# Starting a chunk's first four w_in tiles around the last x matmuls, and loading two w_out rows earlier

## The chip, the cores and the metric

One core of one Trainium2 chip runs the whole program. The metric is the device time in microseconds (us); the profile shows one execution and its span, which is some 1.8 us shorter than the time. A program on one core is timed in rounds: kernel and kernel before on the same chip, in turn.

## The reference, cut to what matters

```python
# q, k, v: (8, 8, 576, 64) float32; w_in: (512, 2048); w_out: (2048, 512)
q_s = softmax(q, axis=-1)                    # over head_dim
k_s = softmax(k, axis=2)                     # over the sequence
kv  = einsum('bhsd,bhse->bhde', k_s, v)      # 64 x 64 for each head
x   = einsum('bhsd,bhde->bhse', q_s, kv)     # then (B*S, H*D) = (4608, 512)
out = gelu_exact(x @ w_in) @ w_out
```

## The kernel before

Batch b's first 512 tokens make chunk b; the rest of all batches make chunk 8. For each chunk TensorE does, in order: kv (72 small 64x64 matmuls, two groups of two head pairs), x (8 matmuls on quarters of the array), h (16 w_in tiles of four 128x128x512 matmuls, each followed by a Gelu on ScalarE) and y (64 w_out matmuls into four banks). The change touches only the seam between chunk 0 and chunk 1. There chunk 0's y runs with the w_out row tiles t outermost, all four banks open, because w_out is still being loaded; the kv and x of batch 1 are put between the last y matmuls:

```python
    for t in range(12):
        y_part(t, range(J))                  # 4 matmuls, one for each y bank
    tp_step(1, 0)
    tp_step(1, 1)
    load(3)
    cast_wo(3, wo[3], 2, 1, "s")             # ScalarE casts row 2, then row 3
    cast_wo(3, wo[3], 3, 1, "s")
    y_part(12, range(J))
    y_part(13, range(J))
    kv_mm(1, 0)                              # 36 matmuls: pairs 0, 1
    kv_norm(1, 0)                            # VectorE: reciprocal, multiply -> kvc
    y_part(14, range(J))
    x_tile(1, 0, psum_a, "a")
    x_tile(1, 1, psum_h, "h")
    x_mm(1, 0)                               # 4 matmuls: pairs 0, 1
    kv_mm(1, 1)
    x_evac(1, 0, "s")                        # "s": ScalarE, else VectorE
    x_evac(1, 1, "s")
    kv_norm(1, 1)
    y_part(15, range(J))
    y_out(0, yps[0], 0)
    y_out(0, yps[1], 1, "s")
    # ... x tiles of pairs 2, 3 ...
    x_mm(1, 1)
    x_evac(1, 2)
    x_evac(1, 3, "s")
    y_out(0, yps[2], 2)
    y_out(0, yps[3], 3)
    h_phase(1, {12: [lambda: cast_v_all(2)]}, groups={0: 2})
```

The last loads of batch 1 and of w_out are issued in this order on one queue:

```python
    wo.append(load_wo(3))                    # its rows 0 and 1
    for hp in range(3):
        load_v1(hp)                          # 288 KB each
    load_wo_row(wo[3], 2)                    # 256 KB: w_out rows of t = 14
    load_v1(3)
    load_wo_row(wo[3], 3)                    # t = 15
```

The softmax here doesn't subtract the row's maximum and nothing guards it: scores larger than these inputs give would overflow.

## Time and profile before

| | before |
|---|---|
| time, median of 3 | 279.8 us (279.69 to 279.89) |
| span of the profiled execution | 278.4 us |
| TensorE (PE) busy | 269.5 us, 97% |
| ScalarE (ACT), VectorE (DVE), GpSimd (POOL) busy | 57%, 36%, 12% |
| all waits that the profile finds for PE | 4.3 us, none between 24 and 50 us |

A timeline line gives start, length, engine, line of the kernel, operation, what is written from what, shapes and the number of instructions merged; in brackets stands how long the engine had been idle and what ended that. The lines themselves are in the prediction.

### The profile page before, as it was taken

Reading aid. Unit: us, or ns where it says so; the run is one execution under the profiler, and the core shown is the slowest. Engines: PE = TensorE matmul, PEld = TensorE weight load, DVE = VectorE, ACT = ScalarE, POOL = GpSimd, SP = SyncE. Lnnn points to the kernel's source line nnn. Section 1 sums busy time; section 2 is a strip of 40 time slices with the busy share of each in tenths; the row PEclk is TensorE's granted clock in tenths of the full one; section 3 lists DMA queues with packets and bytes.
Section 4 is the critical chain, followed back from the end, with each engine's and each line's share of the span. In section 5 each row is a group of like instructions: output and inputs, shape, how many; then the busy total and the mean of one; then the engine's idle time right before and its main releaser. Section 6 shows DMA issues by size and latency. Waiting matters only on the chain.

```text
span 278.4 us, 4542 instructions
## 1 busy us (share of the span) xinstructions
PE 269.5 (97%) x1896; PEld 126.1 (45%) x1924; DVE 100.5 (36%) x151; ACT 158.4 (57%) x246; POOL 33.6 (12%) x25
## 2 busy tenths in 40 slices
PE   7799999999999999999999999999999999999995
PEld 3344454444444444444444444444444444444443
DVE  1877474309753540183008400651015200130012
ACT  3867666689377816691569346943683363136400
POOL 1620050002020220004000500050005000000000
PEclk9999999999999999999999999999999999999999
DMA  7999999963992139702981199117501500120033
GB/s 237 399 403 432 398 398 408 398 250 86 302 348 61 54 110 274 283 38 79 257 343 41 40 228 395 41 56 189 115 0 75 151 2 0 75 78 0 0 78 77
DMA packets 44980, 50.10 MB, mean 180 GB/s; under 512 B 20384, under 2 KB 29856, under 8 KB 44704
## 3 DMA queue, kind: packets, MB, share of 16 engines
q1 hardware_dynamic: 44560, 49.39, 52.9%
q10 hardware_dynamic: 400, 0.43, 0.6%
q8 instruction: 15, 0.25, 0.4%
q14 instruction: 5, 0.04, 0.1%
HBM read 36.70 MB, written 9.44 MB: 166 GB/s over the span
## 4 chain that ended last, share of the span: by engine, by line
PE 94%; DMA 2%; issue 1%; DVE 1%; POOL 1%; ACT 0%; POOLq 0%
PE ps L321 44%; PE ps L331 43%; PE kv L188 2%; DMA f<-in_q_dram 2%; PE ps L278 2%; PE ps L356 1%; POOL e L222 1%; PE pair L321 1%; PE ps L239 1%; ACT e L145 0%; DVE qsum L220 0%; PE ps L283 0%; DVE kvc L202 0%; PE tp L239 0%; PE ps L440 0%
## 5 line engine op out<-in xcount | busy, mean ns | idle before, releaser
L321 PE MATMUL ps<-xT,wi_bf 128*128 128x512 bf16 x557 | 124.2, 379 | 0.6
L331 PE MATMUL ps<-wo_bf,g 128*128 128x512 bf16 x543 | 122.1, 379 | 1.6 <-issue 1.1
L326 ACT ACTIVATE g<-ps 128x512 bf16<-128x512 f32 x142 | 83.7, 597 | 67.4 <-PE ps L321 67.4
L321 PEld LDWEIGHTS <-wi_bf 128*128 128x128 bf16 x576 | 56.2, 98 | 67.9 <-issue 0.2
L331 PEld LDWEIGHTS <-g 128*128 128x128 bf16 x560 | 53.9, 98 | 64.3 <-issue 0.4
L339 DVE COPY y_sb<-ps 128x512 f32<-128x512 f32 x34 | 23.3, 686 | 80.9 <-PE ps L331 77.8
L222 POOL TENSOR_TENSOR e<-e,recq 128x2048 bf16<-128x2048 bf16 (+1 forms) x9 | 25.7, 2856 | 177.6 <-DVE recq L221 149.5
L162 DVE CAST v_aug<-f 128x576 bf16<-128x576 f32 x25 | 17.1, 745 | 47.2 <-DMA f<-in_v_dram 47.2
L220 DVE TENSOR_REDUCE qsum<-e 128x16 f32<-128x1024 bf16 (+1 forms) x13 | 21.0, 1619 | 15.0 <-ACT e L145 15.0
L304 ACT CAST xT<-ps 128x512 bf16<-128x512 f32 x18 | 9.8, 588 | 26.1 <-PE ps L278 16.6
L145 ACT ACTIVATE e<-f 128x512 bf16<-128x512 f32 (+1 forms) x42 | 20.5, 556 | 3.7 <-DMA f<-in_q_dram 3.5
L150 ACT ACTIVATE ek<-f 128x2304 bf16<-128x2304 f32 (+1 forms) x10 | 17.1, 1726 | 0.4 <-DMA f<-in_k_dram 0.4
L302 DVE CAST xT<-ps 128x512 bf16<-128x512 f32 x17 | 11.0, 686 | 17.1 <-PE ps L278 14.1
L79 ACT ACT_TABLE_LOAD x9 | 11.5, 1283 | 2.8 <-issue 2.7
L440 PE MATMUL ps<-zeros 128*128 128x512 f32 (+1 forms) x16 | 8.7, 697 | 1.5 <-DVE zeros L474 1.5
L145 ACT ACT_TABLE_LOAD x7 | 9.0, 1283 | 0.1
L407 DVE CAST wi_bf<-w 128x512 bf16<-128x512 f32 x12 | 7.3, 663 | 2.2 <-DMA w<-in_moe_w_in_dram 1.9
L188 PEld LDWEIGHTS <-ek 64*64 64x64 bf16 x576 | 6.4, 105 | 2.7 <-issue 0.7
L188 PE MATMUL kv<-v_aug,ek 64*64 64x65 bf16 x576 | 6.8, 193 | 0.4 <-DVE kvc L202 0.4
L222 DVE TENSOR_TENSOR e<-e,recq 128x1024 bf16<-128x1024 bf16 x4 | 6.4, 1595 | 0.1
L278 PE MATMUL ps<-qT,kvc 64*64 64x512 bf16 x62 | 5.4, 389 | 0.4 <-DVE kvc L202 0.4
L440 PEld LDWEIGHTS ps<-zeros 128*128 128x128 f32 x14 | 3.3, 244 | 5.4 <-issue 4.0
(39 smaller groups left out, 49.6 us busy)
## 6 DMA issues: line engine op xcount, KB each, us to landing
out_dram<-y_sb SPq DMA_DIRECT2D x32, 256.0 KB, 2.4
f<-in_k_dram SPq DMA_DIRECT2D x6, 1152.0 KB, 9.8
f<-in_v_dram SPq DMA_DIRECT2D x6, 1152.0 KB, 11.6
f<-in_q_dram SPq DMA_DIRECT2D x6, 1024.0 KB, 7.3
w<-in_moe_w_in_dram SPq DMA_DIRECT2D x6, 512.0 KB, 8.9
f<-in_v_dram SPq DMA_DIRECT2D x8, 288.0 KB, 6.6
f<-in_q_dram SPq DMA_DIRECT2D x4, 512.0 KB, 9.1
w<-in_moe_w_out_dram SPq DMA_DIRECT2D x2, 1024.0 KB, 12.5
```

The costliest lines, as they stand in the source:

```text
L79: nc.scalar.activation(out=scr[:, 1:2], in_=scr[:, 0:1], func=func)
L145: nc.scalar.activation(out=dst[:, i], in_=src[:, u], func=AF.Exp)
L150: nc.scalar.activation(out=ek[b % 2][:, i:i + n], in_=st[b]["kf"][:, i:i + n].rearrange("p x (n d) -> p x n d", n=NS), func=AF.Exp,)
L162: eng.tensor_copy(out=o, in_=i)
L188: nc.tensor.matmul(ps[c, place[hp], 0:D + 1], ek[b % 2][pr, hp, n, :], v_aug[b % 2][pr, hp, n, 0:D + 1], start=(n == 0), stop=(n == NS - 1),)
L220: nc.vector.reduce_sum(out=qsum, in_=eq[:, :, hs, :], axis=AX.X)
L222: eng.tensor_tensor(out=eq[:, :, hs, :], in0=eq[:, :, hs, :], in1=recq.unsqueeze(3).to_broadcast([128, J, w, D]), op=ALU.mult,)
L321: nc.tensor.matmul(ps, wi_bf[:, dm, t * 128:(t + 1) * 128], xT[:, dm, :], start=(dm == 0), stop=(dm == NDM - 1),)
L326: nc.scalar.activation(out=g[:, t, :], in_=ps, func=AF.Gelu)
L331: nc.tensor.matmul(ps, st[c]["g"][:, t, j * 128:(j + 1) * 128], wo_bf[:, t, :], start=(t == 0), stop=(t == NDF - 1),)
L339: nc.vector.tensor_copy(out=y_sb, in_=ps)
L440: nc.tensor.matmul(ps, z[:, 0:128], z, start=True, stop=True)
```

## The change

Its intent: give TensorE work of chunk 1 that needs only the first two head pairs, so that the normalization of the other two and the copies of their x lie beside matmuls; and have row 3 of the last w_out block on chip earlier, since two of its matmuls now come earlier. Cut to its core:

```diff
-    for hp in range(3):
+    for hp in range(2):
         load_v1(hp)
     load_wo_row(wo[3], 2)
+    load_wo_row(wo[3], 3)
+    load_v1(2)
     load_v1(3)
-    load_wo_row(wo[3], 3)
 ...
     y_part(14, range(J))
+    y_part(15, (0, 1))
     x_mm(1, 0)
     kv_mm(1, 1)
+    y_out(0, yps[0], 0)
     x_evac(1, 0, "s")
-    x_evac(1, 1, "s")
+    x_evac(1, 1)
     kv_norm(1, 1)
-    y_part(15, range(J))
-    y_out(0, yps[0], 0)
     y_out(0, yps[1], 1, "s")
+    y_part(15, (2, 3))
+    h_begin(1)
+    hps = ...                     # two "h" banks, two "y" banks
+    for t in range(2):
+        h_mm(1, hps[t], t, (0, 1))         # the early w_in matmuls
+    y_out(0, yps[2], 2, "s")
+    y_out(0, yps[3], 3)
     x_mm(1, 1)
-    x_evac(1, 2)
-    x_evac(1, 3, "s")
-    y_out(0, yps[2], 2)
-    y_out(0, yps[3], 3)
-    h_phase(1, {12: [...]}, groups={0: 2})
+    x_evac(1, 2, "s")
+    x_evac(1, 3)
+    for t in range(2, 4):
+        h_mm(1, hps[t], t, (0, 1))
+    for t in range(4):
+        h_mm(1, hps[t], t, (2, 3))
+        h_gelu(1, hps[t], t)
+    h_phase(1, {12: [...]}, t1=4)
```

More of the change, by code (lines that the diff above doesn't have):

```diff
@@ L304, in x_evac, with h_begin, h_mm, h_gelu @@
             nc.scalar.copy(out=st[b]["xT"][:, hp, :], in_=ps)
-    def h_phase(c, ins, groups={}, banks={}):
-        g = moe_sb.tile([128, NDF, M], BF16, tag="g", bufs=1)
-        st[c]["g"] = g
-        xT = st[c]["xT"]
-        t1 = 0
+    def h_begin(c):
+        st[c]["g"] = moe_sb.tile([128, NDF, M], BF16, tag="g", name="g", bufs=1)
+    def h_mm(c, ps, t, dms):
+        for dm in dms:
+            nc.tensor.matmul(
+                ps, wi_bf[:, dm, t * 128:(t + 1) * 128], st[c]["xT"][:, dm, :],
+                start=(dm == 0), stop=(dm == NDM - 1),
+            )
+    def h_gelu(c, ps, t):
+        nc.scalar.activation(out=st[c]["g"][:, t, :], in_=ps, func=AF.Gelu)
+    def h_phase(c, ins, groups={}, banks={}, t1=0):
+        if t1 == 0:
+            h_begin(c)
         while t1 < NDF:
@@ L320, in h_phase @@
                 for ps, t in zip(pss, ts):
-                    nc.tensor.matmul(
-                        ps, wi_bf[:, dm, t * 128:(t + 1) * 128], xT[:, dm, :],
-                        start=(dm == 0), stop=(dm == NDM - 1),
-                    )
+                    h_mm(c, ps, t, (dm,))
             for ps, t in zip(pss, ts):
-                nc.scalar.activation(out=g[:, t, :], in_=ps, func=AF.Gelu)
+                h_gelu(c, ps, t)
                 for f in ins.get(t, []):
@@ L565 @@
     kv_mm(1, 1)
+    y_out(0, yps[0], 0)
     x_evac(1, 0, "s")
-    x_evac(1, 1, "s")
+    x_evac(1, 1)
     kv_norm(1, 1)
-    y_part(15, range(J))
-    y_out(0, yps[0], 0)
     y_out(0, yps[1], 1, "s")
+    y_part(15, (2, 3))
+    h_begin(1)
+    hps = [psum_h.tile([128, M], FP32, tag="h", name="ps") for t in range(2)]
+    hps += [psum_y.tile([128, M], FP32, tag="y", name="ps") for t in range(2)]
+    for t in range(2):
+        h_mm(1, hps[t], t, (0, 1))
+    y_out(0, yps[2], 2, "s")
+    y_out(0, yps[3], 3)
     x_tile(1, 2, psum_a, "a")
@@ L574 @@
     x_mm(1, 1)
-    x_evac(1, 2)
-    x_evac(1, 3, "s")
-    y_out(0, yps[2], 2)
-    y_out(0, yps[3], 3)
-    h_phase(1, {12: [lambda: cast_v_all(2)]}, groups={0: 2})
+    x_evac(1, 2, "s")
[5 more added lines that the diff above has]
+        h_gelu(1, hps[t], t)
+    h_phase(1, {12: [lambda: cast_v_all(2)]}, t1=4)
     exp_q(2, parts=2)
```

## The prediction

> **What bounds the kernel now.** I read first the page's busy times, then the waits of the TensorE alone, then the timeline of 41 to 45.6 us, where chunk 0 ends and chunk 1 begins, because the diff touches nothing else. First the page's row of busy times and two pieces of the chain that ended last in order of time (start, length, what); then every wait that the profile finds for PE, in the whole span:
>
> ```profile
> PE 269.5 (97%) x1896; PEld 126.1 (45%) x1924; DVE 100.5 (36%) x151; ACT 158.4 (57%) x246; POOL 33.6 (12%) x25
> ...
> 28.70 8.42 PE ps L331 x39
> ```
> ```profile
> PE ps L440 <- DVE zeros L474: 1.5, 1, 1.5
> PE ps L331 <- issue: 1.1, 7, 0.2
> PE ps L239 <- POOL e L222: 0.9, 1, 0.9
> PE kv L188 <- DVE kvc L202: 0.4, 1, 0.4
> PE ps L278 <- DVE kvc L202: 0.4, 1, 0.4
> ```
>
> PE is busy 97% of 278.4 us, and all its waits together are 4.3 us: 1.5 + 0.9 + 0.4 + 0.4 of them belong to batch 0's start (before 15 us), and 1.1 to seven pauses of 0.2 us. "Busy" alone would not prove a full pipe, so the rate is checked: 39 matmuls of 512 columns in 8.42 us are 0.216 us each. None of the waits lies between 24 and 50 us. So in the changed stretch the time is the sum of PE's issue intervals, and any gain must come from one of those being longer than it needs to be.
>
> The stretch itself, from the timeline (start, length, engine, line, operation, count; in brackets idle time before it), then a comparison piece from batch 2:
>
> ```profile
> 41.61 0.48 PE L188 MATMUL kv<-v_aug,ek 64*64 64x65 bf16 x36
> 41.65 0.67 POOL L162 CAST v_aug<-f 128x576 bf16<-128x576 f32 x1 [0.73 <-DMA f<-in_v_dram]
> 42.02 1.04 PE L331 MATMUL ps<-wo_bf,g 128*128 128x512 bf16 x3
> 42.25 0.62 ACT L435 CAST wo_bf<-w 128x512 bf16<-128x512 f32 x1 [0.77 <-DMA w<-in_moe_w_out_dram]
> 42.36 0.29 DVE L202 TENSOR_TENSOR kvc<-kv,rec 128x128 bf16<-128x128 f32 x1
> 42.99 0.41 PE L278 MATMUL ps<-qT,kvc 64*64 64x512 bf16 x4
> 43.23 0.51 PE L188 MATMUL kv<-v_aug,ek 64*64 64x65 bf16 x36
> 43.44 1.07 ACT L304 CAST xT<-ps 128x512 bf16<-128x512 f32 x2 [0.58 <-PE ps L278]
> 43.67 1.04 PE L331 MATMUL ps<-wo_bf,g 128*128 128x512 bf16 x4
> 44.01 0.29 DVE L202 TENSOR_TENSOR kvc<-kv,rec 128x128 bf16<-128x128 f32 x1
> 44.22 0.68 DVE L339 COPY y_sb<-ps 128x512 f32<-128x512 f32 x1
> 44.40 0.60 ACT L341 COPY y_sb<-ps 128x512 f32<-128x512 f32 x1
> 44.64 0.40 PE L278 MATMUL ps<-qT,kvc 64*64 64x512 bf16 x1
> 44.64 0.40 PE L278 MATMUL xx<-qT,kvc 64*64 64x512 bf16 x1
> ...
> 44.98 3.84 PE L321 MATMUL ps<-xT,wi_bf 128*128 128x512 bf16 x16
> 45.09 0.69 DVE L302 CAST xT<-ps 128x512 bf16<-128x512 f32 x1 [0.20 <-PE xx L278]
> 45.12 0.59 ACT L304 CAST xT<-xx 128x512 bf16<-128x512 f32 x1
> ```
> ```profile
> 66.52 4.91 PE L331 MATMUL ps<-wo_bf,g 128*128 128x512 bf16 x22 [0.16 <-issue]
> 71.36 0.63 PE L278 MATMUL ps<-qT,kvc 64*64 64x512 bf16 x8
> ```
>
> The reader is to see whether x waits for its kv. It looks as if it could: kvc is ready at 42.65 (42.36 + 0.29) and x starts at 42.99; again 44.30 and 44.64. But the four w_out matmuls ahead of x need 4 x 0.216 + 0.01 (the first one after small matmuls is 0.01 longer) = 0.87 us, and x comes 0.97 us after the first of them, 0.09 to 0.10 more. In batch 2, where kvc was ready long before, 22 w_out matmuls need 22 x 0.216 = 4.75 us, and x comes 71.36 - 66.52 = 4.84 us after the first: the same 0.09. So that 0.09 is a fixed price for going from whole-array matmuls to quarter-array ones, not a wait. Nothing waits here that could be hidden.
>
> **What the Trainium skill says.** "TensorE: Matmul & The Clock Gate", section "Back-to-back issue gap", gives a warm gap of N/2.4 + 2.5 ns, 216 ns for 512 columns; the trace agrees (0.216). "TensorEngine Tiling (Array Packing)", section "Key Properties", says that changing the tiling mode drains the engine; the trace agrees, at 0.09 us for each such entry. "Perfetto Trace Analysis", section "Matmuls", wants independent groups to rotate through PSUM banks so that an evacuation overlaps the next group; the four early w_in tiles do that, and the cost to check is whether their banks are evacuated in time. "DMA: Bandwidth & Descriptors", section "Two DMAs through the same engine are not ordered", says that descriptors of one queue start in order; this is why I take the rows of w_out to land in the order of issue, as rows 2, v 3, row 3 did (casts at 40.86, 41.65, 42.25).
>
> **The change, part by part.** No instruction is added or taken away: 8 w_out matmuls of t = 14 and 15, 8 x matmuls, 72 kv matmuls, 16 matmuls of four w_in tiles, four copies of x, four of y. Only their order differs.
>
> PE before, by starts: kv at 41.61; 0.41 to y14 (42.02); 0.97 to x01 (42.99); 0.24 to kv (43.23); 0.44 to y15 (43.67); 0.97 to x23 (44.64); 0.34 to h (44.98); 16 h matmuls, 16 x 0.216 + 0.01 = 3.46; the fifth w_in tile starts at 48.44.
> PE after: kv at 41.61; 0.41; six y matmuls, 0.97 + 2 x 0.216 = 1.40, x01 at 43.42; 0.24, kv at 43.66; 0.44, the last two y at 44.10; 4 h matmuls from 44.10 + 0.01 + 2 x 0.216 = 44.54; (2 + 4) x 0.216 + 0.10 = 1.40 puts x23 at 45.50; 0.34, h again at 45.84; 12 x 0.216 + 0.01 = 2.60; the fifth tile at 48.44.
> The number of entries into quarter-array mode is the same, so the sum is the same: 0.00 us, if nothing new waits.
>
> Now the new waits, with durations of the same rows; a semaphore takes about 0.05 us (x01 ends at about 43.40, ACT's copy starts at 43.44). Successive copies start 0.48 us apart on ACT (1.07 - 0.59) and 0.60 on DVE (1.28 for two of 0.68 further on in the timeline).
> - ACT: copy of x0 at 43.42 + 0.45 = 43.87, ends 44.46, ready for PE at 44.51; the first early h wants it at 44.54. Fits by 0.03. Copy of y bank 1 at 44.35, ends 44.95, ready 45.00; tile 1's first matmul, which takes that bank, wants it at 44.54 + 2 x 0.216 = 44.97. Late by 0.03. Copy of y bank 2 at 44.83 to 45.43, wanted at 45.84: in time.
> - DVE: y bank 0 is complete at about 43.27, its copy runs 43.32 to 44.00, x1's copy from 43.92 to 44.61, ready 44.66, wanted at 44.76: in time. kv's normalization follows at about 44.53 and ends about 45.03, wanted at 45.50: in time. y bank 3 until about 45.7, wanted at about 46.3: in time.
> - x2 and x3: copies at 45.50 + 0.45 = 45.95 to 46.6, wanted at 45.84 + 0.01 + 4 x 0.216 = 46.71: in time by about 0.1.
> - Loads: row 3 (256 KB) moves ahead of v 3 and v 2, so its cast runs about 1.4 us earlier, near 40.8 to 41.5; it is now wanted at 42.02 + 0.01 + 4 x 0.216 = 42.90, where the old cast end (42.25 + 0.62 = 42.87) would have been on the edge. v 2 and v 3 land some 0.6 us later (256 KB at about 400 GB/s); v 3's cast would then end near 42.32 + 0.6 = 42.9, wanted at 43.66: in time.
> Sum: 0.00 of work + 0.03 of wait = +0.03 us, which PE carries to the end because it never idles later.
>
> **Rivals.** (1) The change hides a wait and gains. The most it could win is the two x stages: 0.34 from x23 to h and 0.10 ahead of it, so 0.4 us, 279.4. Against it: those intervals are the mode change and the streaming of x itself, and remain. (2) Evacuation becomes the bound: ACT now has to copy x0, y1 and y2 in a row beneath 1.4 us of PE work, with margins of 0.03 us. If each copy came 0.1 to 0.2 us later than I place it, PE would stand 0.1 to 0.4 us: about 280.1. For it: the thin margins; against it: ACT is idle before 43.44 and its copies repeat to the nanosecond level. (3) v 2 and v 3 come late by more than their 0.7 us of margin, since the queue is saturated there (about 390 to 410 GB/s): kv and all behind it would slip by 0.3 to 0.8 us, about 280.4. Against it: only 256 KB passes them.
>
> **Range and chances.** Predicted 279.8 us. Runs of before spread over 0.2 us (279.69 to 279.89); rival 1 gives the lower edge, 279.4, and rivals 2 and 3 the upper, 280.3. 2% are 5.6 us; nothing in this stretch is that large, and only an unforeseen lost transfer or a slower chip could do it. Faster 0.005, same 0.98, slower 0.015.
>
> **What would show it.** In the changed trace: the x matmuls of pairs 0 and 1 about 0.43 us later and those of 2 and 3 about 0.86 us later than before; the four early h matmuls ahead of the latter without a gap over 0.05 us; the fifth w_in tile within 0.1 us of 48.44; ACT's cast of row 3 before 42 us; no new row among PE's waits above 0.2 us. I am wrong if the fifth tile starts more than 0.2 us from 48.44 or if a difference arises later than that tile, which would mean that the order of loads or of copies reaches further than I see.

## The result, and the profile after

The changed kernel takes 279.94 us (median of 6, 279.63 to 280.02), before 279.88 us (6 runs). The ratio is 1.0001, 95% interval 0.9988 to 1.0014: the same. A ratio here is the mean time of one kernel's fast runs over that of the other's of the same rounds, so not quite the ratio of the medians.

From the page and the timeline of the changed kernel (its w_out line is now L339, its w_in line L311):

```profile
PE 269.3 (97%) x1896; PEld 126.0 (45%) x1924; DVE 100.4 (36%) x151; ACT 158.3 (57%) x246; POOL 33.5 (12%) x25
```
```profile
39.72 1.26 ACT L443 CAST wo_bf<-w 128x512 bf16<-128x512 f32 x2 [0.66 <-DMA w<-in_moe_w_out_dram]
41.16 1.37 POOL L162 CAST v_aug<-f 128x576 bf16<-128x576 f32 x2 [1.36 <-DMA f<-in_v_dram]
41.29 0.48 PE L188 MATMUL kv<-v_aug,ek 64*64 64x65 bf16 x36
41.70 1.47 PE L339 MATMUL ps<-wo_bf,g 128*128 128x512 bf16 x5
42.99 0.69 DVE L347 COPY y_sb<-ps 128x512 f32<-128x512 f32 x1 [0.66 <-PE ps L339]
43.10 0.41 PE L278 MATMUL ps<-qT,kvc 64*64 64x512 bf16 x4
43.34 0.51 PE L188 MATMUL kv<-v_aug,ek 64*64 64x65 bf16 x36
43.55 0.59 ACT L304 CAST xT<-ps 128x512 bf16<-128x512 f32 x1 [2.57 <-PE ps L278]
43.78 0.60 PE L339 MATMUL ps<-wo_bf,g 128*128 128x512 bf16 x2
44.04 1.08 ACT L349 COPY y_sb<-ps 128x512 f32<-128x512 f32 x2
44.22 0.81 PE L311 MATMUL ps<-xT,wi_bf 128*128 128x512 bf16 x3
44.39 0.29 DVE L202 TENSOR_TENSOR kvc<-kv,rec 128x128 bf16<-128x128 f32 x1
45.18 0.40 PE L278 MATMUL ps<-qT,kvc 64*64 64x512 bf16 x1
45.52 3.20 PE L311 MATMUL ps<-xT,wi_bf 128*128 128x512 bf16 x14
```

PE's rows follow each other without a bracket, as before: nothing waits. (Counts of 5 and 3 where the program has 6 and 4 are missing records.) Everything is some 0.32 us earlier than in the first trace, because chunk 0 itself began earlier. So I measure from the first kv matmul, and use two rulers. The **stretch** runs from the first kv matmul of batch 1 to the first w_out matmul of chunk 1, by the starts of single matmuls: 17.195 us before, 17.195 us after. The **tail** runs from the start of the last matmul to the end of the span. Between the two lie 215.93 or 215.94 us in every trace, so whatever the stretch loses or gains reaches the end.

By step: x01 (pairs 0 and 1) started 1.81 us after the kv group (43.10 - 41.29), before 1.38; x23 at 3.89, before 3.03; the fifth w_in tile at 6.835 in both (by the starts of its first matmul, 48.123 - 41.288 and 48.443 - 41.608).

### The profile page after: what moved, and what is told of

The parts are those of the page before. It is cut to its first block, busy times and chain, and to the rows that moved or that the text cites. A ratio compares the mean times of both kernels' runs of the same rounds, so it can differ in the third digit from the quotient of the medians.

```text
span 278.1 us, 4543 instructions
## 1 busy us (share of the span) xinstructions
PE 269.3 (97%) x1896; PEld 126.0 (45%) x1924; DVE 100.4 (36%) x151; ACT 158.3 (57%) x246; POOL 33.5 (12%) x25
## 4 chain that ended last, share of the span: by engine, by line
PE 92%; DMA 4%; issue 1%; POOL 1%; ACTq 0%; SPq 0%; DVE 0%
PE ps L339 43%; PE ps L311 43%; DMA w<-in_moe_w_in_dram 3%; DMA touch<-in_moe_w_in_dram 2%; PE kv L188 2%; PE ps L278 1%; PE ps L364 1%; PE pair L311 1%; POOL wi_bf L412 1%; PE ps L283 0%; PE ps L239 0%; ACTq L468 0%; PE tp L239 0%; SPq L400 0%; ACTq L101 0%
## 5 line engine op out<-in xcount | busy, mean ns | idle before, releaser
L311 PE MATMUL ps<-xT,wi_bf 128*128 128x512 bf16 x557 | 124.3, 379 | 0.6
L339 PE MATMUL ps<-wo_bf,g 128*128 128x512 bf16 x543 | 122.1, 379 | 1.6 <-issue 1.1
L311 PEld LDWEIGHTS <-wi_bf 128*128 128x128 bf16 x576 | 56.1, 98 | 68.2 <-POOL wi_bf L412 0.8
L339 PEld LDWEIGHTS <-g 128*128 128x128 bf16 x560 | 53.9, 98 | 64.3 <-issue 0.4
L347 DVE COPY y_sb<-ps 128x512 f32<-128x512 f32 x33 | 22.7, 686 | 81.2 <-PE ps L339 78.1
L441 DVE CAST wo_bf<-w 128x2048 bf16<-128x2048 f32 (+1 forms) x4 | 4.4, 1090 | 3.8 <-DMA w<-in_moe_w_out_dram 3.8
```

What stands on the lines that cost most here:

```text
L311: nc.tensor.matmul(ps, wi_bf[:, dm, t * 128:(t + 1) * 128], st[c]["xT"][:, dm, :], start=(dm == 0), stop=(dm == NDM - 1),)
L339: nc.tensor.matmul(ps, st[c]["g"][:, t, j * 128:(j + 1) * 128], wo_bf[:, t, :], start=(t == 0), stop=(t == NDF - 1),)
L347: nc.vector.tensor_copy(out=y_sb, in_=ps)
```

## The experiments

All kernels gave correct outputs. Twelve ran. Here is what the two rulers show in each; "kv" is the start of the first kv matmul, that is, how late PE reached the stretch in that execution:

| run | kv, us | stretch, us | tail, us | time, us (before in the same rounds) |
|---|---|---|---|---|
| before | 41.61 | 17.195 | 3.68 | 279.88 (with the changed kernel) |
| changed kernel | 41.29 | 17.195 | 3.73 | 279.94 (279.88) |
| before_again | 41.13 | 17.197 | 3.70 | 279.75, one run (279.81) |
| loads_only | 41.36 | 17.194 | 3.75 | 280.05, one run (279.81) |
| order_only | 41.26 | 17.679 | 3.70 | 280.35, one run (279.81) |
| no_early_h | 41.14 | 17.614 | 3.71 | 280.17 (279.81), ratio 1.0011, 0.9998 to 1.0025 |
| slow_norm_before | 41.21 | 17.194 | 3.60 | 279.70 (279.82), 0.9992, 0.9979 to 1.0005 |
| slow_norm_after | 41.37 | 17.551 | 3.61 | 280.21 (279.82), 1.0010, 0.9998 to 1.0023 |
| slow_norm2_before | 41.04 | 17.693 | 3.59 | 280.03 (279.81), 1.0006, 0.9994 to 1.0019 |
| slow_norm2_after | 41.26 | 17.412 | 3.61 | 279.85 (279.81), 1.0000, 0.9988 to 1.0013 |
| merged | 41.15 | 18.198 | 4.59 | 281.70 (279.82), 1.0066, 1.0053 to 1.0080 |
| merged2 | 41.13 | 17.138 | 4.55 | 280.59 (279.81), 1.0026, 1.0013 to 1.0040 |
| merged3 | 41.31 | 16.923 | 3.60 | 279.75 (279.82), 1.0000, 0.9988 to 1.0013 |
| two_fewer | 41.14 | 17.356 | 3.69 | 279.81 (279.82), 1.0000, 0.9987 to 1.0014 |

No kernel differs from before by 2%, and of the nine experiments timed in several rounds only merged and merged2 have an interval of the ratio that leaves out 1. All else is told from the traces, whose rulers repeat to 0.003 us where nothing waits.

**The kernel before once more**, no edit.

> The kernel before, unchanged, profiled once more, to see how far its own traces differ. The ruler of all runs here: the interval from the first kv matmul of pairs 0 and 1 of batch 1 to the first matmul of the fifth w_in tile of chunk 1; it was 6.83 us in the trace of before and 6.84 in that of the changed kernel, although the spans were 278.4 and 278.1 us. My theory (PE is full there, so the order does not matter): 6.83 again within 0.01, while the start of that interval (41.61 us in the first trace, 41.29 in the changed kernel's) may move by some tenths, because it hangs on when the first loads land. The rival (the changed kernel really starts chunk 1 0.3 us earlier and loses it elsewhere) expects 41.6 again.

The stretch is 17.197 us and kv starts at 41.13. So the 0.3 us by which the two spans differed are the start of an execution, not the change. The rival is out. It also shows that the first trace (of an execution of 280.19 us, above the three timed runs of its set) was the latest of all 14 to reach the stretch, which matters below.

**The loads alone.**

```diff
-    for hp in range(3):
+    for hp in range(2):
         load_v1(hp)
     load_wo_row(wo[3], 2)
+    load_wo_row(wo[3], 3)
+    load_v1(2)
     load_v1(3)
-    load_wo_row(wo[3], 3)
```

> Only the second part of the change: rows 2 and 3 of the last w_out block are loaded ahead of v pairs 2 and 3, the order of work stays as before. My theory: the interval stays 6.83 us; ScalarE casts the two rows back to back at about 39.7 to 41.0 instead of at 40.9 and 42.2, GpSimd's casts of v 2 and v 3 move to about 41.2 to 42.5, which is still ahead of the second kv group at about 43.2. The rival (the loads alone cost or gain) expects a wait of the kv matmuls on v, 0.2 to 0.6 us, or a gain at the w_out matmuls of t = 15.

The stretch is 17.194. ScalarE cast both rows from 40.10 to 41.35, GpSimd v 2 and v 3 from 41.47 to 42.85, as expected. By itself the new order of loads neither costs nor gains in this trace.

**The order of work alone** (the changed kernel with the loads of before).

> Only the first part of the change: the order of work as in the changed kernel, the loads as before. The two early w_out matmuls of t = 15 now want row 3 about 1.29 us after the first kv matmul; its cast ended 1.26 us after it in the trace of before. My theory: that is on the edge, so the interval is 6.84 us plus a wait of 0.0 to 0.3 us on ScalarE's cast, ahead of t = 15, depending on how the loads lie against PE in that run. The rival (the new order of loads does nothing) expects 6.84 and no such wait.

From its timeline, ScalarE's cast of row 3 and the two early w_out matmuls of t = 15:

```profile
42.37 0.62 ACT L443 CAST wo_bf<-w 128x512 bf16<-128x512 f32 x1 [0.76 <-DMA w<-in_moe_w_out_dram]
43.04 0.59 PE L339 MATMUL ps<-wo_bf,g 128*128 128x512 bf16 x2 [0.33 <-ACT wo_bf L443]
```

The cast ends at 42.99 and the matmul starts at 43.04; the stretch is 0.48 us longer. The mechanism is as expected, the size above my 0.0 to 0.3: I had taken kv's distance to the loads from the first trace, where PE was late and so had more slack. The second part of the change is what makes the first one free.

**The early w_in matmuls put behind x23**, all else as in the changed kernel.

```diff
-    for t in range(2):
-        h_mm(1, hps[t], t, (0, 1))
     y_out(0, yps[2], 2, "s")
     y_out(0, yps[3], 3)
     # ...
     x_mm(1, 1)
     x_evac(1, 2, "s")
     x_evac(1, 3)
+    for t in range(2):
+        h_mm(1, hps[t], t, (0, 1))
```

> The changed kernel with the four early w_in matmuls (tiles 0 and 1, pairs 0 and 1) moved behind the x matmuls of pairs 2 and 3. In the changed kernel these x matmuls come 1.84 us after the second kv group starts, and kvc is ready for them 1.39 us after it (end of its normalization 1.34, plus 0.05). Without the four matmuls (0.86 us) PE would be there after 0.98 us. My theory: x waits 0.4 us for kvc, the interval is 6.84 + 0.41 = 7.25 us, and the time is 0.4 us longer than before (0.15%, at the edge of what the rounds can resolve). The rival (a wait is not what these matmuls cover; the change is neutral because nothing in it matters) expects 6.84 us and no wait on the normalization.

```profile
44.59 0.40 PE L278 MATMUL ps<-qT,kvc 64*64 64x512 bf16 x1 [0.35 <-DVE kvc L202]
```

Now x23 waits for kvc, and the stretch is longer by 0.419 us; 0.41 was expected. (The bracket counts from the modelled end of the matmul before, so it shows less than the delay.) So the four matmuls do hide a wait. But that wait exists only because the change took two w_out matmuls away from in front of x23 and put y0's copy and x1's copy ahead of the normalization. In the kernel before, four w_out matmuls covered a shorter wait with 0.29 us to spare. The sum agrees: two matmuls less are 0.43 us, kvc came 0.27 later after the second kv group, and 0.43 + 0.27 - 0.29 = 0.41.

**A slower normalization, before and after: two useless VectorE copies ahead of it.**

```diff
+    for _ in range(2):
+        nc.vector.tensor_copy(out=zeros, in_=zeros32)
     kv_norm(1, 1)
```

> The kernel before with two useless VectorE copies of 128x512 (zeros into a tile of zeros that nothing reads any more; some 0.3 us each, call their sum d, about 0.7) ahead of the normalization of kv pairs 2 and 3: the suspected cost, made larger. In before, kvc is ready 0.29 us ahead of the x matmuls that want it. My theory: x is late by d - 0.29, about 0.4 us; the copy of y bank 0, which follows the normalization on VectorE and whose bank the first w_in tile takes, then ends d later as well and holds that tile by some further 0.2 us, so that the interval is 6.83 + 0.4 to 0.7 us. The rival (PE has more slack here than the order of work shows) expects 6.83.

> The same two copies in the changed kernel, at the same place ahead of the normalization of pairs 2 and 3. Here kvc is ready 0.45 us ahead of the x matmuls, and the copy of y bank 0 comes before the normalization. My theory: x is late by d - 0.45, about 0.25 us, nothing further, so the interval is 6.84 + 0.25 us and the changed kernel beats the other with the same load by 0.2 to 0.45 us: what the change buys is slack, which the kernel before did not need. The rival (the change moves work about and gives no slack) expects both to lose the same.

The first one failed as an experiment. VectorE's timeline in slow_norm_before:

```profile
42.17 0.88 DVE L569 CAST zeros<-zeros 128x512 bf16<-128x512 f32 x2
43.41 0.17 DVE L201 RECIPROCAL rec<-kv 128x2 f32<-128x2 f32 x1 [0.36 <-PE kv L188]
```

The copies ran in VectorE's idle time before kv was there, and the reciprocal still waited 0.36 us for PE: no delay, stretch 17.194. In the changed kernel VectorE is busy ahead of the normalization, so there they did delay kvc, by 0.80 us, and the stretch grew by 0.356; that fits the 0.45 us that kvc had been early there (0.80 - 0.45 = 0.35). The pair does not compare the slack of the two kernels, since the same code was not the same load. I repeated it with the copies where they cannot slip ahead.

**The same two copies inside the normalization.**

```diff
         nc.vector.reciprocal(rec[:, 0:m], src[:, :, D])
+        if b == 1 and half == 1:
+            for _ in range(2):
+                nc.vector.tensor_copy(out=zeros, in_=zeros32)
         nc.vector.tensor_tensor(
```

> The kernel before with the two useless VectorE copies (0.45 us each, as measured in the last pair) put between the reciprocal and the multiplication of the normalization of kv pairs 2 and 3, so that they cannot slip into VectorE's idle time ahead of it, as they did in slow_norm_before. d is 0.90 us. My theory: kvc comes 0.90 later; it was 0.29 early, so x of pairs 2 and 3 is late by 0.61. The copy of y bank 0 stands behind the normalization on VectorE and ends at 44.90 + 0.90 + 0.05 by the clock of the first trace, while the first w_in matmul, which takes that bank, wants it at 44.98 + 0.61: another 0.26. Sum +0.87 us on the interval from the first kv matmul to the first w_out matmul of chunk 1, which was 17.20 in before, after, loads_only and slow_norm_before alike. The rival (nothing in this stretch matters to PE, whatever its order) expects 17.20.

> The same two copies at the same place in the changed kernel. My theory: kvc comes 0.90 later and was 0.45 early, so x is late by 0.45; the copy of y bank 0 comes ahead of the normalization here, and the w_in tiles that follow x want their y banks only later, so nothing is added: 17.20 + 0.45 = 17.65 us. The changed kernel would then beat the other by 0.42 us under the same load (0.15%, seen in the traces to 0.01 us and in the rounds just so). The rival expects both to lose the same.

First the copy of y bank 0 and the x23 matmul in slow_norm2_before, then the x23 matmul in slow_norm2_after:

```profile
44.43 0.68 DVE L342 COPY y_sb<-ps 128x512 f32<-128x512 f32 x1
44.57 0.40 PE L281 MATMUL ps<-qT,kvc 64*64 64x512 bf16 x1 [0.30 <-ACT y_sb L344]
```
```profile
45.37 0.40 PE L281 MATMUL ps<-qT,kvc 64*64 64x512 bf16 x1 [0.36 <-DVE kvc L205]
```

The copies overlapped the reciprocal, so the multiplication came 0.66 us later, not 0.90. With 0.66 the theory gives 0.66 - 0.29 = 0.37 us before and 0.66 - 0.45 = 0.21 after. After: 0.217 measured. Before: x23 was 0.374 late, and 0.137 more was lost ahead of it, at the first w_out matmul of t = 14, which waited for ScalarE's cast of row 2 (cast end 41.54, matmul 41.59; without a wait it comes 0.41 after the first kv matmul, at 41.45): the old order of loads, in an execution where PE arrived early. Together 0.51; the stretch grew by 0.498. The bracket in the first fence names ScalarE, but ScalarE had long been done with what x23 needs; the normalization ended at 44.51, 0.06 before x23. My further 0.26 us for y bank 0 did not come: the first w_in matmul starts at 44.91 while that bank's copy runs to 45.11, so it does not take that bank. So the changed kernel does have 0.16 us more slack at x23. With this load its stretch is 0.28 us shorter, 0.16 of it from that slack and the rest from row 2; in time that is 0.18 us between medians, with overlapping intervals.

**A version with fewer changes between whole-array and quarter-array matmuls.**

```diff
     kv_mm(1, 0)
-    kv_norm(1, 0)
+    kv_mm(1, 1)
+    kv_norm(1)
     y_part(14, range(J))
-    y_part(15, (0, 1))
+    y_part(15, (0,))
     # ... (cut: banks of x2 and x3, place of kvc)
     x_mm(1, 0)
-    kv_mm(1, 1)
-    # ... copies, normalization ...
-    y_part(15, (2, 3))
-    # ... early w_in matmuls ...
     x_mm(1, 1)
+    # ... copies ...
+    y_part(15, (1, 2, 3))
+    # ... w_in tiles 0, 1, 2 in the three "h" banks, then h_phase(1, ..., t1=3)
```

> A version of my own with the fewest entries into quarter-array mode: both kv groups in a row with one normalization, five w_out matmuls over it, all eight x matmuls in a row, the other three w_out matmuls, then the w_in tiles; loads as in the changed kernel. From intervals of the trace of before: 72 kv matmuls to the next w_out 0.94 us, then 5 x 0.216 + 0.10 = 1.18, eight x matmuls to the next w_out 0.56 (both as in later chunks), 3 x 0.216 + 0.01 = 0.66, 16 x 0.216 = 3.45: 6.79 us, so 0.04 us less than either kernel, if the copies keep their places; that is below what the rounds resolve, and the trace has to show it. The rival (each entry saved gives back its 0.1 us in full) expects 6.6 us.

It is slower by 1.9 us. Its kv matmuls:

```profile
41.92 0.22 PE L188 MATMUL kv<-v_aug,ek 64*64 64x65 bf16 x2 [0.29 <-POOL v_aug L162]
42.61 0.48 PE L188 MATMUL kv<-v_aug,ek 64*64 64x65 bf16 x34 [0.47 <-POOL v_aug L162]
```

The second kv group now comes right behind the first and waits for the casts of v 2 and v 3, which the changed kernel loads last. The next w_out matmul starts 1.87 us after the first kv matmul, 1.16 later than in merged3 below, where nothing waits; 0.11 more is lost at a w_in matmul that waits for x3's copy (copy end 46.56, matmul 46.61). Less the 0.27 that merged3 will show to be saved, that is the stretch's 1.0 us. The other 0.9 us are in the tail, where nothing was changed.

> My merged version without the two faults that its trace showed: its second kv group waited 1.2 us for GpSimd's cast of v 3, because v 2 and v 3 are loaded last in the changed kernel, so here all four v pairs are loaded ahead of rows 2 and 3; and the copies of x2 and x3 ran one after the other on two engines, so here ScalarE takes both, and VectorE the y banks. My theory: no wait is left, 0.04 us below either kernel: 17.15 us instead of 17.20. The cost of an entry into quarter-array mode is mostly hidden, since 36 kv matmuls take 0.41 to 0.44 us to the next w_out matmul and 72 take 0.94. The rival (each of the two entries saved gives back 0.1 us) expects 17.0. Its last output writes landed 0.9 us later than in all other runs, after the last matmul, with an instruction fetch among them; if that comes from the length of the program, it is here again, and the time is 280.7 rather than 279.8.

The edit against merged, cut (the order of the matmuls of w_in tiles 0 and 1 and the engines of two more y copies change too):

```diff
-    for hp in range(2):
+    for hp in range(HP):
         load_v1(hp)
     load_wo_row(wo[3], 2)
     load_wo_row(wo[3], 3)
-    load_v1(2)
-    load_v1(3)
 ...
-    y_out(0, yps[0], 0, "s")
     x_evac(1, 0)
     x_evac(1, 1, "s")
-    x_evac(1, 2)
+    x_evac(1, 2, "s")
     x_evac(1, 3, "s")
+    y_out(0, yps[0], 0)
```

The stretch is 17.138, about my 17.15, but for a wrong reason: the first w_out matmul of t = 14 waited there too, for row 2's cast, which ended at 42.02 (matmul at 42.07). The next run shows the stretch without that wait. The tail is long again, 4.55 us.

**The tail: the same kernel with four useless VectorE memsets in chunk 5.** In all traces there is one last instruction fetch of 8192 bytes. Where VectorE has 196 instructions (those of its sequencer counted) it starts 0.6 us after the last matmul's start; with 198, 2.0 us ahead of it; with 194 (merged, merged2), 2.1 to 2.2 us after it, when the last output writes are on their way, and these then land 0.4 to 0.9 us later than elsewhere.

```diff
+        if c == 5:
+            for _ in range(4):
+                nc.vector.memset(zeros[:, 0:2], 0.0)
```

> merged2 with four useless two-element VectorE memsets in chunk 5, where VectorE idles; nothing else. In the ten traces so far the last instruction fetch of 8192 bytes goes with VectorE's instruction count: 196 (before, after) fetch 0.6 us after the last matmul's start, span ends 3.70 us after it; 198 (both slow_norm pairs) fetch 2.0 us ahead of it, end 3.60; 194 (merged, merged2) fetch 2.1 us after it, among the last output writes, end 4.57. My theory: with 198 the fetch is out of the way again and the tail is 3.60, while the interval from the first kv matmul of batch 1 to the first w_out matmul of chunk 1 stays at merged2's 17.14: span about 277.9 minus what the start gives or takes, time 279.65, 0.9 below merged2 and 0.15 below before. The rival (the late landing has to do with merged2's order of work) expects the tail of 4.55 and 280.6 again.

The queue's own waits for the output writes, in merged2 and then in merged3 (us in total, times, longest):

```profile
SPq L671 <- DMA out_dram<-y_sb: 2.4, 2, 1.6
```
```profile
SPq L674 <- DMA out_dram<-y_sb: 1.5, 2, 1.2
```

The tail is 3.60 us, with the fetch 2.04 us ahead of the last matmul: as expected, and the order of work that the rival blamed is the same in both. The traces also tell how the writes are late. A write leaves sixteen marks as it lands. In merged and merged2, fifteen marks of the last write came by 2.82 and 2.80 us after the last matmul's start, like the last mark of all in the other traces (2.69 to 2.85), and the sixteenth at 3.69 and 3.65; of each of the two writes ahead of it one mark is late too. The fetch ran from 2.17 to 2.48 and from 2.13 to 2.49, and SyncE's output packets, which had stopped at 2.12 and 2.16, went on at 2.48 and 2.49. So one sixteenth of these writes was held up, and it went on when the fetch ended. The stretch, though, is 16.923, not 17.14:

```profile
41.31 0.78 PE L188 MATMUL kv<-v_aug,ek 64*64 64x65 bf16 x72
42.02 1.25 PE L339 MATMUL ps<-wo_bf,g 128*128 128x512 bf16 x5
```

72 kv matmuls take 0.71 us to the next w_out matmul. My 0.94 came from a trace in which the record of the first w_out matmul after kv was missing, so it was one matmul (0.22) too long. The kernel before enters quarter-array mode three times here (kv; x with kv; x), merged3 twice. One entry saved, with its exit, is thus worth 0.27 us (17.195 - 16.923). My expectations for merged and merged2 count two entries saved; that was a miscount. The rival of merged2 (17.0) was nearer than I. Its median is 0.07 us below before, its lowest run 279.53 (before 279.72), its highest 280.33. The traced run is one of the fast ones; I have no trace of a slow one, so why they spread stays open, and merged3 is not shown to beat either kernel.

**The tail in the kernel before: two output copies of chunk 5 given to ScalarE.**

```diff
-            y_out(c, ps, j)
+            y_out(c, ps, j, "s" if c == 5 and j in (1, 3) else "v")
```

> The kernel before with two of its output copies of chunk 5 done by ScalarE instead of VectorE, where ScalarE idles: VectorE has 194 instructions, and the order on TensorE, on the loads and in the changed stretch is untouched. My theory: the last fetch falls among the last output writes, the tail from the last matmul's start is 4.57 instead of 3.70 us, and the time is 0.87 us longer than before, 280.7. The rival expects 279.8.

A miss: 279.81 us, tail 3.69. VectorE lost not two instructions but four (192): two of its sequencer went with the copies. The last fetch then comes 4.3 us after the last matmul's start, behind the last landing at 2.7, and delays nothing. That fits a fetch that moves with the count, but the test I wanted, 194 in another kernel, was not made. Its stretch is 0.16 longer, once more row 2: ScalarE's cast of it ended at 41.68, and the first w_out matmul of t = 14 started at 41.73; without a wait its place was 41.56.

## Why the prediction was right, point by point

- **PE is full, so reordering gives 0.00.** Right to the resolution of the trace: stretch 17.195 and 17.195. There was no wait to remove. No_early_h and slow_norm2 show that the mechanism behind the change is real (0.419 and 0.217 us where waits were made) and that the kernel before simply had cover enough. PE was even fuller than I read it: the seven pauses of 0.2 us ("issue") are missing records. Behind the kv group at 65.59 the program has 23 w_out matmuls to the next x and the prediction's line 22; merged3's trace has all 23 there, and no such pause anywhere:

```profile
65.73 5.14 PE L339 MATMUL ps<-wo_bf,g 128*128 128x512 bf16 x23
```

- **The 0.09 us in front of x is a price, not a wait.** Right: w_out to x takes 0.306 to 0.310 us in every trace where kvc is early, and 0.684 or 0.728 where it is late. That the number of mode changes decides fits merged3. As a figure for what a saved entry is worth, 0.09 is too small: merged3 gives 0.27 for one entry with its exit. Of this, 0.14 lies in kv: 72 matmuls in a row reach the next w_out matmul after 0.71 us, two groups of 36 need 0.41 and 0.44.
- **A wait of 0.03 us on y bank 1.** It did not come: tile 1's first matmul started in its place, 44.655, and the copy had ended at 44.627. A matmul that waits for a copy starts some 0.05 after its end, so tile 1 seems not to take that bank, but this is not shown; in the kernel before the bank that I assumed for the first tile was wrong (slow_norm2_before). The step is mis-sized by 0.03 us.
- **Loads in time.** Right for the changed kernel: v 3's cast ends 1.24 us after the first kv matmul, wanted at 2.05; row 3's cast ended before kv began. Incomplete for the kernel before: I read row 2's slack at t = 14 (0.5 us) from the one trace in which PE came latest. In six traces with the old order of loads it is -0.18 to 0.5 us, and in two of them PE waits, 0.14 and 0.18 us; in the five traces with the changed kernel's loads, merged apart, it is at least 0.89. So the change of loads does gain something in some executions; the medians show none of it.
- **Rivals 2 and 3** did not occur in the changed kernel. In merged, rival 3's mechanism (v too late) cost 1.16 us, because the cover was taken away.
- **The signs it named.** The steps came as stated when counted from the first kv matmul: x01 0.43 later, x23 0.86. By the letter, one sign failed: the fifth w_in tile was to start within 0.2 us of 48.44 and started at 48.12, because that execution reached the stretch 0.32 earlier. A sign tied to the clock of one trace was badly chosen: in before_again the same kernel moved by 0.47.

## What to carry to other kernels

Hiding a latency gains only what is waited for at present: before moving work in front of a dependent instruction, subtract the time at which its input is ready from the time at which the engine gets there, in more than one trace. When work is moved away from one wait to cover another, and when a later instruction is moved ahead, its loads have to move with it, as order_only and merged show. If a small reordering changes the time by more than its own stretch shows, look at the two ends of the span before inventing a reason.

## What the Trainium skill lacked or had wrong

- "TensorE: Matmul & The Clock Gate", section "Back-to-back issue gap", also says that in a real kernel 512-column matmuls sustain some 131 ns each. Here they come every 215 to 216 ns (39 in 8.42 us), its figure for an isolated one, which is the one that the prediction cites.
- "TensorEngine Tiling (Array Packing)", section "Key Properties", says that a mode change drains the engine, but gives no size. Here the entry shows as 0.093 us in front of the first small matmul, and one entry fewer (with its exit) saved 0.27 us.
- "Runtime: NRT & Kernel Launch", section "Instruction fetch mechanics", calls the cost of crossing a block of instructions mostly hidden. Here the last fetch is not hidden where it falls among the last output writes: tails of 4.55 and 4.59 us against 3.59 to 3.75 in all other traces, back to 3.60 after four useless VectorE instructions. No page says that the number of an engine's instructions can move the end of a kernel by 0.9 us. That the fetch holds up one sixteenth of the writes rests on the times in two traces; a fetch moved among the last writes of another kernel was not tried with success.
